# One core, linear attention and mixture of depths: late stores, first steps, gate sums and the last rows rearranged

## The chip, the cores and the metric

The kernel runs on one core of a Trainium2 chip. The metric is the device time of one execution in microseconds (us), lower is better. TensorE (PE) multiplies, its weight loads are shown as PEld; VectorE is DVE, ScalarE is ACT, GpSimd is POOL, and SyncE (SP) only issues transfers. All five run their own instruction queues in program order and wait for each other on semaphores.

## The reference

```python
# attention: B=4 batches, H=8 heads, S=768 positions, D=64, blocks of 64
for b in range(nb):
    intra = einsum('bhic,bhjc->bhij', qb, kb) * Dmask      # Dmask[i,j] = lam**(i-j), i >= j
    intra = einsum('bhij,bhjd->bhid', intra, vb)
    inter = einsum('bhid,bhde->bhie', qb * lam_pow, kv_state)
    out[:, :, sl] = intra + inter
    kv_state = lam_block * kv_state + einsum('bhsd,bhse->bhde', kb * rev_pow, vb)
x = out.transpose(0, 2, 1, 3).reshape(B, S, 512)
# mixture of depths: 128 of the 768 rows of each batch, by score, go through an expert
scores = einsum('bsd,d->bs', x, w_gate)
top_idx = argpartition(-scores[b], capacity)[:capacity]
xe = x[b, top_idx]
out[b, top_idx] = xe + sigmoid(scores[b, top_idx])[:, None] * (relu(xe @ w1) @ w2)
```

All is float32; w1 is 512x1024 and w2 1024x512.

## The kernel before, in words

The sequence is cut into 24 steps g of 128 positions, six to a batch (`NT` = 6). The order of all instructions is written out by hand in one loop over g from -1 to 23; a helper adds the waits. Step g works on the outputs of g and prepares g+1: `transposes(g+1)` turns q and k on PE (ACT copies them out of PSUM), `queries_decayed` and `keys_decayed` scale them on POOL, `scores(g+1)` makes the score blocks in the PSUM tile `su`, `masked` multiplies them by the decay mask on DVE, `state_products` and `next_state` carry the state (`decay_state` scales the old state on POOL), `from_scores(g)` and `from_states(g+1)` accumulate the output in the PSUM tile `o_`, and `outputs(g)` copies it on ACT to `x_b`, from which `store(g)` sends it to DRAM. Steps 0 to 7 are wide (`WIDE` = 8: a state per 128 positions), later ones narrow (two blocks of 64).

Each step also routes: `gate_scores(g)` sums x times the gate vector on DVE, `row` turns the sums into a row (PE, ACT), `compare` fills a table on DVE, `column_sums` counts on PE. When a batch is complete, `find` marks the hits (DVE), `take` makes the token numbers (`tokens`: PE, DVE) and gathers the 128 rows of the batch from DRAM on POOL's queue (`fetch`). Three steps after a batch's last, its expert enters a list of 17 pieces: `gate` (four transposes and a copy `xsT`), eight `hidden` and eight `back`; `products(n)` takes n of them. `finish` makes y and scatters it to DRAM on POOL's queue.

SP's queue holds all loads and stores in program order: at each step the loads of step g+3 (three of 256 KB), then weights (`W1_AT`, `W2_AT`: eight of 512 KB), then the late stores. The outputs of steps 6 to 11 are kept back by

```python
LATE_STORES = {11: (6, 7), 12: (8, 9), 13: (10, 11)}
```

and the fetch of batch 1, in step 13, reads the rows of batches 0 and 1 from DRAM, so it waits for these stores.

Of the kernel before, what the change touches and what calls it, by code (L numbers as in the profile page):

```python
# [17 lines left out]
def kernel(  # L18
# [12 lines left out]
    nc = tc.nc  # L31
# [20 lines left out]
    LATE_STORES = {11: (6, 7), 12: (8, 9), 13: (10, 11)}  # L52
    PIECES = {8: 2, 14: 2, **{g: 2 for g in range(16, 23)}}
# [56 lines left out]

    mask_w = const.tile([128, 2, NHP, L], FP32, name="mask_w")
# [25 lines left out]
    def narrow_constants():  # L137
# [4 lines left out]

    su = psum.tile([128, 2, 512], FP32, name="su")
    o_ = psum.tile([128, 2, 512], FP32, name="o")
    Q_BANK, K_BANK, U_BANK, SMALL = (psum.tile([128, 512], FP32, name=f"m{i}") for i in range(4))
    free = [Q_BANK, K_BANK, U_BANK, SMALL]
    held = []
    nc.vector.memset(
        su[half[1]].rearrange("p a (b i) -> p a b i", i=L)[:, :, :, :C], 0.0
    )  # L150

    def bank(hold=False):
        t = next(t for t in free if not any(t is x for x in held))
        free[:] = [x for x in free if x is not t] + [t]
        if hold:
            held.append(t)
        return t
# [41 lines left out]
    def queries_decayed(g):  # L199
        if g >= NG:  # L200
            return
# [101 lines left out]
    def from_states(g):  # L303
        if g >= NG:
            return
        qs = qss.pop(g)
# [63 lines left out]
    def gate_scores(g):  # L370
        b, t = divmod(g, NT)
        xg = mod.tile([128, HD], FP32, name="xg")
        if wide(g):
            nc.vector.tensor_tensor_reduce(
                out=xg[:].rearrange("p (a m) -> p a m", a=2), in0=o_[:, :, : NHP * D],
                in1=wg_o[:].rearrange("p (a m) -> p a m", a=2),
                scale=1.0, scalar=0.0, op0=ALU.mult, op1=ALU.add,
                accum_out=scs[b][:, t : t + 1],
            )
            return  # L380
# [100 lines left out]
    def expert(b, i):  # L481
# [3 lines left out]
        def gate():  # L485
# [8 lines left out]
            nc.scalar.copy(out=xsT[:].rearrange("p a b -> p (a b)"), in_=pt[:])  # L494
# [55 lines left out]

        return [gate] + [hidden(f) for f in range(NFC)] + [back(f) for f in range(NFC)]
# [7 lines left out]
    wg_o = const.tile([128, HD], FP32, name="wg_o")  # L559

    def gate_vector():
        nc.tensor.matmul(SMALL[:], lhsT=one_row[:], rhs=wg_row[:], start=True, stop=True)
        nc.scalar.copy(
            out=wg_o[:].rearrange("p (a b e) -> p a b e", a=2, e=D),
            in_=SMALL[:].rearrange("p (b a e) -> p a b e", a=2, e=D),
        )
        nc.scalar.copy(out=wg_b[:], in_=SMALL[:])

    def constants():
# [187 lines left out]
```

## Time and profile before

| | us |
|---|---|
| median of 3 timed runs | 194.16 (193.62 to 194.2) |
| the profiled execution's own time | 192.19 |
| its span in the trace | 190.4 |
| PE busy | 160.2 |
| DVE busy, POOL busy, ACT busy | 97.9, 94.2, 71.9 |

The profiled execution is 1.97 us below the median of the timed runs; 1.8 us of its time lie outside the span. Times in the rows below count from the start of the span. A matmul in float32 shows as two instructions.

### The profile page before, as it was taken

What the parts mean: (1) busy time and instruction counts of PE and PEld (TensorE: products, weight loads), DVE (VectorE), ACT (ScalarE), POOL (GpSimd) and SP (SyncE); (2) the same over time, 40 slices, a digit from 0 to 9 for tenths busy, and PEclk for the clock granted to TensorE, in tenths of its full rate; (3) what the DMA queues carried; (4) which work ended last, traced back from release to release, by engine and by line L of the source; (5) the groups of instructions that cost most, each with busy time, mean ns of one, the idle gap of its engine ahead of it and who ended that gap; (6) DMA issues with size and microseconds to landing.
All of it is one profiled execution on the core that took longest, in us unless ns stands there. A gap on an engine that the chain in (4) does not pass through costs nothing.

```text
span 190.4 us, 7792 instructions
## 1 busy us (share of the span) xinstructions
PE 160.2 (84%) x3422; PEld 127.8 (67%) x3422; DVE 97.9 (51%) x227; ACT 71.9 (38%) x193; POOL 94.2 (49%) x103
## 2 busy tenths in 40 slices
PE   0797989999669997999248899997999889989990
PEld 0476879889559896665147789966667779449630
DVE  1946546667746523647052855669665963320000
ACT  2232464453345634523204465544544535012100
POOL 2297646466882743683076384775788400211002
PEclk9999999999999999999957999999999999999996
DMA  5998999998999999999898369898301311011001
GB/s 110 221 218 169 220 213 199 250 222 186 246 314 192 256 293 299 244 257 254 230 254 170 98 129 220 216 242 211 94 34 59 114 59 55 0 55 59 0 0 55
DMA packets 82355, 31.96 MB, mean 168 GB/s; under 512 B 75665, under 2 KB 77713, under 8 KB 82322
## 3 DMA queue, kind: packets, MB, share of 16 engines
q1 hardware_dynamic: 81536, 29.37, 67.2%
q0 software_dynamic: 640, 2.10, 3.3%
q8 instruction: 27, 0.44, 1.0%
q14 instruction: 6, 0.05, 0.1%
q10 hardware_dynamic: 146, 0.01, 0.0%
HBM read 24.12 MB, written 7.34 MB: 165 GB/s over the span
## 4 chain that ended last, share of the span: by engine, by line
PE 38%; issue 17%; DVE 15%; POOL 12%; DMA 10%; ACT 4%; SPq 1%; POOLq 1%; DVEq 0%; ACTq 0%
PE m L530 9%; PE m L518 7%; PE m L192 5%; DVE table L411 4%; POOL decayed L281 4%; PE o L311 4%; PE o L331 3%; DMA xs<-out_dram,tok 3%; PE o L323 2%; PE su L268 2%; POOL kd L176 2%; POOL qs L204 2%; DMA out_dram<-x_b 2%; DMA qn<-in_q_dram 2%; PE su L226 2%
## 5 line engine op out<-in xcount | busy, mean ns | idle before, releaser
L518 PE MATMUL m<-xsT,w_sb 128*128 128x128 f32 x256 | 32.1, 279 | 2.7 <-ACT xsT L494 2.7
L206 POOL TENSOR_TENSOR qs<-qT,qpow 128x512 f32<-128x512 f32 x16 | 21.3, 1328 | 23.5 <-ACT qT L196 23.4
L518 PEld LDWEIGHTS m<-xsT,w_sb 128*128 128x128 f32 x256 | 30.0, 192 | 4.0 <-ACT xsT L494 3.6
L530 PE MATMUL m<-w_sb,hs 128*128 128x512 f32 x64 | 29.7, 598 | 0.0
L411 DVE SCALAR_TENSOR_TENSOR table<-sc_row,sc,lead 128x128 bf16<-128x128 f32 (+5 forms) x24 | 27.0, 1123 | 3.3 <-ACT sc_row L404 3.2
L300 DVE TENSOR_TENSOR state<-su,decayed 128x256 f32<-128x256 f32 x27 | 11.4, 424 | 28.6 <-POOL decayed L281 21.5
L281 POOL TENSOR_TENSOR decayed<-state,decay 128x256 f32<-128x256 f32 x27 | 23.6, 874 | 3.9 <-DVE state L300 2.0
L192 PE MATMUL m<-ident,qn 128*128 128x128 f32 x96 | 16.1, 294 | 6.1 <-DMA qn<-in_q_dram 6.1
L196 ACT COPY qT<-m 128x512 f32<-128x512 f32 x24 | 14.0, 584 | 16.6 <-PE m L192 16.1
L530 PEld LDWEIGHTS m<-w_sb,hs 128*128 128x128 f32 x64 | 11.4, 193 | 9.9 <-issue 9.9
L522 ACT ACTIVATE hs<-m 128x128 f32<-128x128 f32 x32 | 8.9, 279 | 22.5 <-PE m L518 22.5
L311 PE MATMUL o<-state,qs 64*64 64x64 f32 x672 | 16.0, 228 | 1.3 <-ACT x_b L361 0.7
L226 PE MATMUL su<-qT,kT 64*64 64x64 f32 x512 | 10.9, 225 | 7.2 <-DVE state L300 7.2
L176 POOL TENSOR_TENSOR kd<-kn,kpow 128x512 f32<-128x512 f32 x16 | 16.7, 1043 | 0.0
L311 PEld LDWEIGHTS o<-state,qs 64*64 64x64 f32 x672 | 13.1, 138 | 4.9 <-issue 4.0
L204 POOL TENSOR_TENSOR qs<-qT,qpow 128x512 f32<-128x512 f32 x8 | 10.9, 1358 | 10.9 <-ACT qT L196 9.5
L547 POOL DMA_INDIRECT out_dram<-y,tok x4 | 4.2, 1060 | 23.8 <-DVE y L543 23.8
L192 PEld LDWEIGHTS m<-ident,qn 128*128 128x128 f32 x96 | 11.2, 149 | 6.6 <-issue 6.4
L192 PE MATMUL m<-ident,kn 128*128 128x128 f32 x96 | 15.3, 285 | 0.0
L476 POOL DMA_INDIRECT xs<-out_dram,tok x4 | 4.1, 1031 | 22.5 <-DVE tok L459 14.4
L404 ACT COPY sc_row<-m 128x128 f32<-128x128 f32 x24 | 6.4, 267 | 23.2 <-PE m L401 23.2
L226 PEld LDWEIGHTS su<-qT,kT 64*64 64x64 f32 x512 | 9.4, 140 | 7.6 <-DVE state L300 6.3
(79 smaller groups left out, 257.3 us busy)
## 6 DMA issues: line engine op xcount, KB each, us to landing
kn<-in_k_dram SPq DMA_DIRECT2D x24, 256.0 KB, 5.1
qn<-in_q_dram SPq DMA_DIRECT2D x24, 256.0 KB, 5.3
vn<-in_v_dram SPq DMA_DIRECT2D x24, 256.0 KB, 5.6
out_dram<-x_b SPq DMA_DIRECT2D x24, 256.0 KB, 3.8
w_sb<-in_moe_w_dram SPq DMA_DIRECT2D x8, 512.0 KB, 6.1
xs<-out_dram,tok POOLq DMA_INDIRECT x4, 4.3
out_dram<-y,tok POOLq DMA_INDIRECT x4, 3.0
lam_b<-in_lam_dram ACTq DMA_DIRECT2D x1, 4.0 KB, 3.3
```

The costliest lines, as they stand in the source:

```text
L176: nc.gpsimd.tensor_tensor(out=kd[:], in0=loaded[g][0][:], in1=pw[:].rearrange("p a b -> p (a b)").unsqueeze(2).broadcast_to([128, H, D]), ...
L192: nc.tensor.transpose(tp[:, hp * L : (hp + 1) * L], in_=t[:, 2 * hp : 2 * hp + 2, :], identity=ident[:])
L196: nc.scalar.copy(out=dst[:].rearrange("p a i -> p (a i)"), in_=tp[:])
L204: nc.gpsimd.tensor_tensor(out=qs[:], in0=qTs[g][:], in1=qpow[:], op=ALU.mult)
L206: nc.gpsimd.tensor_tensor(out=qs[:].rearrange("p a (c i) -> p a c i", c=2), in0=qTs[g][:].rearrange("p a (c i) -> p a c i", c=2), in1=qpow ...
L226: nc.tensor.matmul(su[half[c], hh, hp * C : (hp + 1) * C], lhsT=kT[half[hh], hp, half[c]], rhs=qT[half[hh], hp, half[c]], start=True, stop ...
L281: nc.gpsimd.tensor_tensor(out=t[:], in0=states[n][:], in1=(decay_w if wide(g) else decay)[:], op=ALU.mult)
L300: nc.vector.tensor_tensor(out=new[:], in0=u, in1=decayed.pop(n)[:], op=ALU.add)
L311: nc.tensor.matmul(o_[half[c if wide(g) else hh ^ c], hh, hp * D : (hp + 1) * D], lhsT=qs[half[hh], hp, half[c]], rhs=states[n][half[hh], ...
L411: nc.vector.scalar_tensor_tensor(out=table[:, : (t + 1) * L], in0=rows_[b][:, : (t + 1) * L], scalar=scs[b][:, t : t + 1], in1=lead[:, (NT ...
L518: nc.tensor.matmul(ph, lhsT=w1_sb[:, dc, f * 128 : (f + 1) * 128], rhs=keep["xsT"][:, dc, :], start=(dc == 0), stop=(dc == NDC - 1),)
L530: nc.tensor.matmul(py[:], lhsT=keep["hs"][:, f, :], rhs=w2_sb[:, f, :], start=(f == 0), stop=(f == NFC - 1),)
```

## The change

The late stores go one step up and ahead of that step's loads. The fetch is split from `take` (as `get`) and stands behind the decay of the state. At the start, 9 matmuls of zeros are issued, `scores(0)` and `masked(0)` go ahead of the first `state_products`, and the gate vector and the routing tables go to later steps; decayed queries of a batch's first wide step are no longer made. In the wide steps the gate sums are taken from the copied rows `x_b` rather than from `o_`, behind `next_state`; `find` goes behind `gate_scores`. Pieces move: none in step 8 but the gate, one more in 14, 20 and 23. The last expert copies `xsT` on two engines and makes and scatters its output in two halves of 256 columns.

```diff
-    LATE_STORES = {11: (6, 7), 12: (8, 9), 13: (10, 11)}
-    PIECES = {8: 2, 14: 2, **{g: 2 for g in range(16, 23)}}
+    LATE_STORES = {10: (6, 7), 11: (8, 9), 12: (10, 11)}
+    PIECES = {8: 0, 14: 2, **{g: 2 for g in range(16, 23)}}
...
+    for _ in range(9):
+        nc.tensor.matmul(SMALL[:, :L], lhsT=zero[:], rhs=zero[:], start=True, stop=True)
...
     def queries_decayed(g):
-        if g >= NG:
+        if g >= NG or (wide(g) and g % NT == 0):
             return
...
     def gate_scores(g):
-        if wide(g):
-            nc.vector.tensor_tensor_reduce(
-                out=xg[:].rearrange("p (a m) -> p a m", a=2), in0=o_[:, :, : NHP * D],
-                in1=wg_o[:].rearrange("p (a m) -> p a m", a=2),
...
         nc.vector.tensor_tensor_reduce(
             out=xg[:], in0=x_bs[b][:, t].rearrange("p a b e -> p (a b e)"), in1=wg_b[:],
...
-            nc.scalar.copy(out=xsT[:].rearrange("p a b -> p (a b)"), in_=pt[:])
+            if last:
+                pv = pt[:].rearrange("p (a b) -> p a b", b=128)
+                nc.scalar.copy(out=xsT[:, : NDC // 2], in_=pv[:, : NDC // 2])
+                nc.vector.tensor_copy(xsT[:, NDC // 2 :], pv[:, NDC // 2 :])
...
+        def half_finish(c):
+            cs = slice(c * (HD // 2), (c + 1) * (HD // 2))
+            y = mod.tile([128, HD // 2], FP32, name="y_half")
+            nc.vector.scalar_tensor_tensor(
+                out=y[:], in0=keep["py"][:, : HD // 2], scalar=keep["g"][:],
+                in1=xss[b, i][:, cs], op0=ALU.mult, op1=ALU.add,
+            )
+            nc.gpsimd.indirect_dma_start(
+                out=rows_upto(b).rearrange("r (c e) -> (r c) e", c=2),
+                out_offset=bass.IndirectOffsetOnAxis(ap=keep["at"][:, c : c + 1], axis=0),
+                in_=y[:], in_offset=None,
+            )
+        if last:
+            after.append(half_rows)
+            return (
+                [gate] + [hidden(f) for f in range(NFC)] + [flush]
+                + [half_back(f, c) for c in range(2) for f in range(NFC)]
+            )
...
     for g in range(-1, NG):
+        for s in LATE_STORES.get(g, ()):
+            store(s)
         loads_to(g + ahead(g))
         for do in weights.get(g, []):
             do()
-        for s in LATE_STORES.get(g, ()):
-            store(s)
...
         if wide(g):
             queries_decayed(g + 1)
+            if g == 0:
+                gate_vector()
             if NGR:
                 compare(g - 1)
-                if ends(g - 2):
-                    take((g - 2) // NT)
             if g >= 0:
                 from_scores(g)
                 outputs(g)
-                gate_scores(g)
                 if g not in kept:
                     store(g)
             if NGR:
+                if ends(g - 2):
+                    take((g - 2) // NT)
+                    get((g - 2) // NT)
                 column_sums(g - 1)
-                if ends(g - 1):
-                    find((g - 1) // NT)
             if g < 0:
-                gate_vector()
-                constants()
-                keys_decayed(1)
+                scores(0)
+                masked(0)
             state_products(g + 1)
             next_state(2 * g + 2)
-            scores(g + 1)
-            masked(g + 1)
+            if g >= 0:
+                gate_scores(g)
+                scores(g + 1)
+                masked(g + 1)
+            if NGR and ends(g - 1):
+                find((g - 1) // NT)
...
+            if g == 0:
+                compare_constants()
             if g == 1:
                 narrow_constants()
+                slot_constants()
+            if g == 3:
+                slot_casts()
             continue
+        if g == NG - 1:
+            products(1)
         from_states(g)
         settle(g)
         queries_decayed(g + 1)
+        if ends(g - 3):
+            for i in range(NGR):
+                pieces.extend(expert((g - 3) // NT, i))
+            if g > WIDE:
+                products(1)
         state_products(g + 1)
         if NGR and ends(g - 2):
             take((g - 2) // NT)
         next_state(2 * g + 2)
         decay_state(2 * g + 3)
+        if NGR and ends(g - 2):
+            get((g - 2) // NT)
         keys_decayed(g + 2)
...
         if NGR:
             column_sums(g - 1)
+        if g == WIDE:
+            products(1)
         outputs(g)
...
         masked(g + 1)
+        gate_scores(g)
         if NGR and ends(g - 1):
             find((g - 1) // NT)
-        gate_scores(g)
         flush()
```

`half_back(f, c)` is `back(f)` for one half of the columns with a PSUM bank of its own per half; `half_rows` makes the row numbers 2*tok and 2*tok+1 on DVE. `compare_constants`, `slot_constants` and `slot_casts` are `constants` cut in three.

## Rows read from the trace of the kernel before

**Rows 1.** Stretches: length, busy us (count) PE, PEld, DVE, ACT, POOL; PEclk; DMA; GB/s.

```profile
20.00:50.00 30.00, 28.27 (x765) 25.10 (x763) 19.17 (x43) 14.32 (x31) 18.49 (x18) 1.00 0.97 223
50.00:97.60 47.60, 37.41 (x903) 29.48 (x895) 21.74 (x54) 18.23 (x54) 26.01 (x26) 0.98 1.07 258
97.60:102.40 4.80, 4.76 (x105) 4.25 (x105) 3.25 (x6) 1.33 (x3) 2.02 (x3) 0.53 1.21 239
102.40:185.20 82.80, 77.32 (x1477) 59.45 (x1473) 41.68 (x97) 32.30 (x97) 36.38 (x36) 1.00 0.38 98
```

**Rows 2.** Timeline, the first 20 us: start, length, instruction, idle time before it.

```profile
6.08 1.09 PE L192 MATMUL m<-ident,qn 128*128 128x128 f32 x4 [6.08 <-DMA qn<-in_q_dram]
...
7.96 2.07 PE L562 MATMUL m<-wg_row,one_row 1*128 1x512 f32 x2
...
8.06 0.59 ACT L196 COPY kT<-m 128x512 f32<-128x512 f32 x1 [0.27 <-PE m L192]
...
11.01 1.98 PE L219 MATMUL su<-qT,kT 64*64 64x128 f32 x32
...
12.66 0.58 DVE L581 CAST slot<-slot_i 128x768 f32<-128x768 int32 x1 [2.43 <-POOL slot_i L578]
...
15.69 1.15 PE L323 MATMUL o<-vn,p 128*64 128x64 f32 x32 [1.47 <-DVE p L236]
...
19.14 0.60 PE L192 MATMUL m<-ident,qn 128*128 128x128 f32 x4
```

**Rows 3.** Timeline of one wide step (g = 3 to 4).

```profile
31.41 1.04 POOL L176 TENSOR_TENSOR kd<-kn,kpow_w 128x512 f32<-128x512 f32 x1
...
32.79 1.23 DVE L236 TENSOR_TENSOR p<-su,mask_w 128x1024 f32<-128x1024 f32 x1
...
34.24 1.01 PEld L323 LDWEIGHTS o<-vn,p 128*64 128x64 f32 x32 [0.17 <-DVE p L236]
```

**Rows 4.** The gate sums' two lines: duration ns min/median/max, first and last start.

```profile
L374 DVE CUSTOM_DVE_ANT_0 xg<-o,wg_o x8: 690/692/692, 17.5 to 50.1; 128x512 f32<-128x512 f32 x8
...
L381 DVE CUSTOM_DVE_ANT_0 xg<-x_b,wg_b x16: 674/682/1754, 59.5 to 159.0; 128x512 f32<-128x512 f32 x16
```

**Rows 5.** Timeline around steps 7 and 8.

```profile
48.33 1.15 PE L323 MATMUL o<-vn,p 128*64 128x64 f32 x32 [0.53 <-DVE p L236]
...
51.33 0.69 PE L226 MATMUL su<-qT,kT 64*64 64x64 f32 x32 [1.22 <-DVE state L300]
...
55.08 0.66 PE L489 MATMUL m<-ident,xs 128*128 128x128 f32 x4 [0.84 <-DMA xs<-out_dram,tok]
```

**Rows 6.** PE's waits over the span: us in total, times, longest.

```profile
PE m L192 <- DMA qn<-in_q_dram: 6.1, 1, 6.1
PE m L518 <- ACT xsT L494: 2.7, 4, 0.7
```

**Rows 7.** Timeline of steps 13 and 14.

```profile
95.39 0.98 POOL L476 DMA_INDIRECT xs<-out_dram,tok  x1 [7.07 <-DMA out_dram<-x_b]
...
97.64 1.13 PE L226 MATMUL su<-qT,kT 64*64 64x64 f32 x32 [5.98 <-DVE state L300]
```

**Rows 8.** The chain that ended last: the last late store, start and length.

```profile
90.76 3.76 DMA out_dram<-x_b
```

**Rows 9.** Timeline of steps 19 and 23, one place each.

```profile
133.00 0.29 PE L401 MATMUL m<-ident,sc 128*128 128x128 f32 x1 [1.23 <-DVE two L457]
...
153.44 0.69 PE L311 MATMUL o<-state,qs 64*64 64x64 f32 x32 [0.71 <-ACT x_b L361]
```

**Rows 10.** Timeline of the end.

```profile
178.15 7.03 PE L530 MATMUL m<-w_sb,hs 128*128 128x512 f32 x16
...
185.22 0.75 DVE L543 SCALAR_TENSOR_TENSOR y<-m,g,xs 128x512 f32<-128x512 f32 x1 [6.12 <-PE m L530]
186.25 0.99 POOL L547 DMA_INDIRECT out_dram<-y,tok  x1 [14.21 <-DVE y L543]
```

**Rows 11.** Page, part 6: gathers of the fetch, median us from issue to landing.

```profile
xs<-out_dram,tok POOLq DMA_INDIRECT x4, 4.3
```

More of the change, by code (lines that the diff above doesn't have):

```diff
@@ L109, with bank @@
     nc.gpsimd.memset(one_row[:], 1.0)
+    su = psum.tile([128, 2, 512], FP32, name="su")
+    o_ = psum.tile([128, 2, 512], FP32, name="o")
+    Q_BANK, K_BANK, U_BANK, SMALL = (psum.tile([128, 512], FP32, name=f"m{i}") for i in range(4))
+    free = [Q_BANK, K_BANK, U_BANK, SMALL]
+    held = []
+    nc.vector.memset(
+        su[half[1]].rearrange("p a (b i) -> p a b i", i=L)[:, :, :, :C], 0.0
+    )
+    def bank(hold=False):
+        t = next(t for t in free if not any(t is x for x in held))
+        free[:] = [x for x in free if x is not t] + [t]
+        if hold:
+            held.append(t)
+        return t
+    for _ in range(9):
+        nc.tensor.matmul(SMALL[:, :L], lhsT=zero[:], rhs=zero[:], start=True, stop=True)
     mask_w = const.tile([128, 2, NHP, L], FP32, name="mask_w")
@@ L141, in narrow_constants @@
         nc.scalar.copy(out=decay[:], in_=qpow[:, :, C - 1 : C].broadcast_to([128, NHP, D]))
[L143 to L157, printed above, removed]
     qTs, qss, kTs, kds, ps_ = {}, {}, {}, {}, {}
@@ L479, in fetch, with expert @@
         xss[b, i] = xs
-    def expert(b, i):
+    def expert(b, i, last=False):
         n_in = min(128, CAP - i * 128)
@@ L549, in finish, with half_back, do, half_rows @@
             )
+        def half_back(f, c):
+            def do():
+                if f == 0:
+                    keep["py"] = bank()
+                nc.tensor.matmul(
+                    keep["py"][:, : HD // 2], lhsT=keep["hs"][:, f, :],
+                    rhs=w2_sb[:, f, c * (HD // 2) : (c + 1) * (HD // 2)],
+                    start=(f == 0), stop=(f == NFC - 1),
+                )
+                if f + 1 == NFC:
+                    half_finish(c)
+            return do
+        def half_finish(c):
[9 more added lines that the diff above has]
+                in_=y[:], in_offset=None,
+            )
+        def half_rows():
+            keep["at"] = at = mod.tile([128, 2], I32, name="half_at")
+            for c in range(2):
+                nc.vector.tensor_scalar(
+                    out=at[:, c : c + 1], in0=toks[b, i][:], scalar1=2.0, scalar2=float(c),
+                    op0=ALU.mult, op1=ALU.add,
+                )
+        if last:
[3 more added lines that the diff above has]
+                + [half_back(f, c) for c in range(2) for f in range(NFC)]
+            )
         return [gate] + [hidden(f) for f in range(NFC)] + [back(f) for f in range(NFC)]
@@ L591, in constants, with slot_casts @@
             )
+    def slot_casts():
+        nc.vector.tensor_copy(slot[:], slot_i[:])
+        nc.vector.tensor_copy(place[:].rearrange("p g c -> p c g"), place_i[:])
     pieces = []
@@ L677 @@
         queries_decayed(g + 1)
+        if ends(g - 3):
+            for i in range(NGR):
+                pieces.extend(expert((g - 3) // NT, i))
+            if g > WIDE:
+                products(1)
         state_products(g + 1)
@@ L682 @@
         decay_state(2 * g + 3)
+        if NGR and ends(g - 2):
+            get((g - 2) // NT)
         keys_decayed(g + 2)
-        if ends(g - 3):
-            for i in range(NGR):
-                pieces.extend(expert((g - 3) // NT, i))
         n = PIECES.get(g, 3)
@@ L690 @@
             row(g - 1)
-        products(1)
+        products(min(n, 1))
         next_state(2 * g + 3)
@@ L695 @@
             compare(g - 1)
-        products(1)
+        products(min(n, 1))
         from_scores(g)
@@ L717 @@
         take(B - 1)
+        get(B - 1)
         products(len(pieces))
@@ L720 @@
         for i in range(NGR):
-            pieces.extend(expert(B - 1, i))
+            pieces.extend(expert(B - 1, i, last=True))
             products(len(pieces))
```

25 lines of the change are left out of this document (9 added, 16 removed).

## The prediction

> **What bounds the kernel now.** I read the stretches first. From the first transposes at 6.08 to the last matmul at 185.2 [rows 2, 10] PE is the engine that does most, and what it loses there is unevenly spread: 1.7 us idle of 30 in the wide steps, 10.2 of 47.6 from 50 on, 5.5 of 82.8 in the late part [rows 1]. In 97.6 to 102.4 PE is full but at a granted clock of 0.53, nearly the lower level of 1.2 GHz [rows 1]. So the kernel is mostly PE's own work with a few holes, and a change pays where it closes one.
>
> Next the timeline, for the holes. The largest is in step 13: POOL waits 7.07 us at 95.39 with the fetch of batch 1, until a store has landed; the decay of the state is queued behind it, the next state behind that, and PE's score products wait 5.98 us for the state [rows 7]. The chain of waits names the store: the last late one, issued at 90.76, landed 3.76 later at 94.52 [rows 8]. Then the start: PE stands until q arrives at 6.08, and the transposes of step 2, the first part of a regular pace, come at 19.14 [rows 2]. Smaller ones stand at steps 7 and 8 [rows 5], before the hidden products (four times 0.7) [rows 6], in steps 19 and 23 [rows 9], and behind the last matmul, where a y of 0.75 and a scatter follow one another [rows 10].
>
> DMA must be kept beside it: 0.97 share in the wide steps and 1.07 from 50 to 97.6 [rows 1]. Up to the stall's end transfers are as full as PE, so what is saved there must not ask for bytes sooner than they can come.
>
> **The change part by part, against the profiled execution's 192.19 us** (span 190.4 and 1.8 around it; the timed median is 1.97 higher).
>
> *Late stores and fetch.* In SP's order the store of step 11 now stands ahead of the loads of steps 15 and 16 and the store of 12, which it used to follow: seven transfers of 256 KB, 1.84 MB, at 258 GB/s [rows 1] 7.1 us. It lands near 94.5 - 7.1 = 87.4 instead of 94.5, before anything is gained earlier. The fetch could go as soon as the token numbers exist, and 95.39 less its wait of 7.07 is 88.3 [rows 7]. So its wait goes; and were 1 or 2 us left, the decay that PE's state needs now stands ahead of it on POOL, with only the keys' decay and the next decay behind. PE's hole of 5.98 closes. With it goes the low clock: 4.76 us of PE work at 0.53 [rows 1] would take about 2.5 at full, 2.3 less. Against that one more piece falls into step 14, a `back`, two of 16 instructions in 7.03 [rows 10], 0.9 us. Sum -7.4. Late next are the loads of steps 13 to 15, behind two, four and six stores, 1.0 us each at that rate: up to 6 us later in the queue. The keys' decay uses them one step after their issue, PE two steps after, so I count nothing, and 4.4 lost at most. Bounds -8.3 and -3.
>
> *The start.* Now 13.06 us pass from the first transposes to those of step 2 (6.08 to 19.14). DVE is held by the cast of the slot table, which itself waited 2.43 us for POOL, and PE's products from scores wait for the masked scores behind it [rows 2]. In the new order the masked scores need besides the decay constants only the score products, and those the second copy, done at 8.65 [rows 2]. At today's speed PE had all its earlier work behind it at 15.69 - 1.47 = 14.22; with the 0.6 that it now waits for the copy that is 14.9 for the products from scores instead of 15.69. At full speed from 8.65 on, score products (1.98 now) and gate vector (2.07 now) take 1.0 each, the next transposes 1.1, the state products 0.6: 12.3. Full speed from 6.08 on moves the copy too: 11.5. That is 0.8, 3.4 and 4.2 earlier, and the rest to step 2 keeps its 3.45. What decides is PE's speed: four transposes take 1.09 at 6.08 and 0.60 at 19.14 [rows 2], although the granted clock is 1.00 in every record of the first stretch. The zero matmuls (18 instructions of 0.22 to 0.27 by the slow row, 4 to 5 us) fit into the 6.08 us in which PE is idle, and give it activity that much sooner. I take -3.0; bounds -4.2 and -0.8.
>
> The Trainium skill (TensorE: Matmul & The Clock Gate, Part 1) says that the throttled clock is the default and that activity releases it; the slow first row agrees, the granted clock shown there does not. By it the zero matmuls bring the fast rows forward and this term lies at its upper end, near -4.
>
> *Gate sums from copied rows.* From `o_` (PSUM) the eight wide sums take 690 to 692 ns, always. The same sum from `x_b`, both inputs in SBUF, takes 682 in the median but 1754 once [rows 4], where it overlapped a POOL multiplication. In a wide step the sum, now behind the state, comes while `kd` runs on POOL to 32.45, so it ends near 33.1 and the masking after it, 1.23 long, at 34.4 instead of 34.0; PE waits for it at 34.24 [rows 3]. That is 0.1 to 0.2 lost per step: +0.7 over seven steps; bounds 0 and +6 (each held as long as the longest shown, 1.07 less the 0.2 of slack).
>
> The Trainium skill (GPSIMD Engine Reference, 1. Specifications) says why: GpSimd shares its SBUF interfaces with VectorE, and they collide where DVE has two SBUF inputs. It speaks against this part, and the one sum of 1754 agrees.
>
> *Tables later.* The cast takes DVE 0.58 [rows 2], the smaller one I put at the same, with a hold of 1.07 at most: 1.2 to 2.2 us once, in step 3, where 1.6 of 4.4 are free (DVE is busy 19.2 of 30 [rows 1]): +0.3; bounds 0 and +0.6. The tables' filling on POOL is covered by POOL's idle time (busy 18.5 of 30 [rows 1]); without it decayed queries would come later by as much.
>
> *Steps 7 and 8.* The masking of 7 no longer stands behind the hits (0.53), the state of step 8 no longer behind a gate sum that waits for its copy (most of 1.22), the gate's transposes come at the end of step 8 and no longer wait for the fetch (0.84), and the first hidden product is a step behind its gate (0.7) [rows 5, 6]: 3.3 at most. But with fewer pieces in step 8 its own chain (decayed queries, decay, state, scores) has less cover, so I take two thirds: -2.2; bounds -3.3 and -1.
>
> *The late steps.* One more wait of 0.7 for `xsT` goes where gate and hidden fall into two steps, and a piece fills the 0.71 in step 23 [rows 6, 9]. The two pieces moved ahead are missing behind the last fetch: a gather lands 4.3 us after its issue [rows 11], six `back` of 0.88 covered it with 5.3 us, and four with 3.5 don't, so 0.8 is lost. Where batches end, gate sum and hits change places; the one behind meets the decayed queries on POOL, and PE waits for it as it did for the other, 1.23 [rows 9]: nothing, by bounds of -2.4 and +1. Sum -0.6; bounds -3 and +1.
>
> *The end.* A half copy of `xsT` saves some 0.25 of the wait of 0.7 [rows 6]; a y of 256 columns takes near half of 0.75 [rows 10], and the first half's scatter goes out 3.5 us before the second. -0.5; bounds -1.0 and 0 (both halves write one tensor, so the second may wait for the first to land).
>
> Sum: -7.4 - 3.0 + 0.7 + 0.3 - 2.2 - 0.6 - 0.5 = -12.7, so 179.5 for a profiled execution, and 194.16 - 12.7 = 181.5 for the median.
>
> **Rivals.** *Transfers give back the early gains.* The start and steps 7 and 8 gain 5.2 us, but DMA is 0.97 busy in the wide steps, 0.9 us free in 30 [rows 1], and full to 97.6. For it: these shares. Against: of all loads only the first ever made PE wait [rows 6]. Then 186.7.
>
> *The wait only changes its place.* Loads that stand behind six stores come late to steps 13 to 15, or the store still lands after the fetch is due. For it: the DMA share of 1.07, a queue that is never empty [rows 1]. Against: the bytes moved behind the store, 7.1 us of them. Then 7.4 becomes about 1 and the time 188.
>
> *It ends slower: the gate sums hold the wide steps.* Each sum could lie behind decayed queries, keys and decay in a row, some 3 us of POOL (`kd` alone 1.04 [rows 3]). It decides when a wide step loses 12.7/8 = 1.6 us; the longest hold shown, 1.07, is not enough [rows 4]. At 2 us a step it is 194.16 - 12.7 + 16 = 197.5. By the Trainium skill's rule on the shared interface it could be so; by the rows it hardly can.
>
> *More is gained.* At batch ends PE's 1.2 us twice [rows 9] goes too, and the start runs at full speed: 177.5.
>
> **How the numbers follow.** Forecast 0.60 (its own range 179 to 184), early gains given back 0.18, wait moved 0.10, more gained 0.09, slower 0.03. The predicted time is 181.5. From 177 to 187 the forecast, the more and most of the given back lie inside, about 0.83. A change within 0.3% (0.6 us) is about what a measurement of this kernel can't tell from none; faster is all but the slower case and 0.01 between: 0.96, 0.01, 0.03.
>
> **What would show it.** In the profile after: the fetch of batch 1 waits under 2 us, and PE's idle time near it stays under 2 with a granted clock of 1.00 throughout; transposes of step 2 at 15 to 17.5, wide steps of 4.4 to 4.6 (sums above 1 us show the held interface); POOL's `kd` in steps 12 to 14 with no wait for a load; behind the last matmul 4.7 instead of 5.2 us. I am wrong if PE waits for loads in steps 9 to 14, if wide steps grow past 5 us, or if the stall stays.

## The result and the profile after

The changed kernel takes 186.77 us in the median of four timed runs (185.32 to 189.67); the kernel before, timed beside it, 194.18. The ratio is 0.961 with a 95% interval of 0.955 to 0.966: faster, by some 4%. The forecast was 181.5, within 177 to 187. So direction and range held, the range by 0.2 us, and the number was 5.3 us too good. The profiled execution takes 185.32 (span 183.5) against 192.19: 6.87 gained where 12.7 were forecast.

Where they went shows when the two traces are cut at the first transposes of a step, in each. Starts are read from the timeline of PE, in us; the last column is the prediction's sum, put on the same stretches. Its -0.6 for the late steps (waits in steps 22 and 23, less the loss behind the last fetch) stands in the last row.

| stretch | before | after | difference | predicted |
|---|---|---|---|---|
| up to the transposes of step 2 | 19.14 | 15.33 | -3.8 | -3.0 |
| steps 1 to 6 | 27.49 | 28.12 | +0.6 | +1.0 |
| steps 7 to 9 | 18.55 | 19.35 | +0.8 | -2.2 |
| steps 10 to 12 | 20.21 | 19.27 | -0.9 | 0 |
| steps 13 and 14 | 21.28 | 14.64 | -6.6 | -7.4 |
| steps 15 to 21 | 40.05 | 44.89 | +4.8 | 0 |
| step 22 and behind | 43.69 | 41.95 | -1.7 | -1.1 |

Two rows carry the miss: steps 7 to 9, 3.0 worse than forecast, and steps 15 to 21, where the sum had nothing but a batch end, put at 0. The -0.9 of steps 10 to 12 lies in step 11, where the trace of the kernel before has a wait of 1.15 us on "issue", of a kind that changes its place from trace to trace (last section); I don't count it as a gain of the change.

The stretches of the changed kernel (the first is steps 1 to 6, then 8 and 9, 13 and 14, 15 to 21; columns as in [rows 1]):

```profile
core 0: us, PE busy (x) PEld busy (x) DVE busy (x) ACT busy (x) POOL busy (x), PEclk, DMA share, GB/s
15.33:43.45 28.12, 26.27 (x694) 23.28 (x694) 21.96 (x43) 13.00 (x28) 20.33 (x23) 1.00 0.99 227
48.17:62.80 14.63, 10.60 (x306) 9.37 (x305) 6.91 (x18) 6.09 (x19) 9.84 (x12) 1.00 1.10 260
82.07:96.71 14.64, 12.59 (x307) 8.97 (x304) 7.72 (x18) 5.93 (x16) 8.86 (x10) 1.00 0.97 230
96.71:141.60 44.89, 40.46 (x1032) 31.66 (x1028) 26.55 (x62) 20.95 (x60) 27.96 (x28) 1.00 0.65 160
```

The granted clock is 1.00 in all four; the 4.76 us at 0.53 that followed the stall [rows 1] have no counterpart. PE is idle 4.0 us of 14.6 in steps 8 and 9, and 4.4 of 44.9 in steps 15 to 21.

The start, against [rows 2] (timeline of PE):

```profile
6.20 0.66 PE L195 MATMUL m<-ident,qn 128*128 128x128 f32 x4 [0.89 <-DMA qn<-in_q_dram]
8.02 1.10 PE L222 MATMUL su<-qT,kT 64*64 64x128 f32 x32 [0.73 <-ACT kT L199]
9.79 0.66 PE L195 MATMUL m<-ident,qn 128*128 128x128 f32 x4
15.33 0.60 PE L195 MATMUL m<-ident,qn 128*128 128x128 f32 x4
```

q still arrives at 6.20, but the first four transposes take 0.66 instead of 1.09 and the score products 1.10 instead of 1.98. Step 13, against [rows 7], first POOL's timeline, then PE's:

```profile
86.71 0.73 POOL L284 TENSOR_TENSOR decayed<-state,decay 128x256 f32<-128x256 f32 x1 [1.98 <-DVE state L303]
87.59 0.99 POOL L471 DMA_INDIRECT xs<-out_dram,tok  x1
```

```profile
85.60 0.30 PE L447 MATMUL m<-place,hit 128*128 128x2 bf16 x6 [1.37 <-DVE hit L437]
```

The fetch goes 0.15 us after the decay, with no wait for a store where it had 7.07. What PE still waits for in this step is 1.37 for the hits. One load does come late: in step 12 POOL's `kd` waits 0.66 us for its keys, at 80.03, where the prediction expected no such wait.

Steps 8 and 9 on PE, against [rows 5, 6], with POOL's part of step 8 in the second fence:

```profile
50.51 0.69 PE L271 MATMUL su<-vn,kd 64*64 64x64 f32 x32 [0.68 <-DVE state L303]
53.69 0.69 PE L229 MATMUL su<-qT,kT 64*64 64x64 f32 x32 [2.01 <-DVE state L303]
56.99 0.27 PE L314 MATMUL o<-state,qs 64*64 64x64 f32 x2 [0.92 <-ACT x_b L364]
```

```profile
50.54 0.73 POOL L284 TENSOR_TENSOR decayed<-state,decay 128x256 f32<-128x256 f32 x1 [0.54 <-DVE state L303]
51.23 1.27 POOL L209 TENSOR_TENSOR qs<-qT,qpow 128x512 f32<-128x512 f32 x1
52.45 0.72 POOL L284 TENSOR_TENSOR decayed<-state,decay 128x256 f32<-128x256 f32 x1
```

A narrow step needs two states in a row, each a decay on POOL and a sum on DVE, and the decayed queries stand between. With no piece in step 8 but the gate at its end, PE waits for the chain twice.

Steps 15 to 21 lose time in two ways. On POOL the scatter of batch 0 now comes ahead of the decayed queries of step 16; on PE two waits end on "issue", that is on nothing that the profile shows another engine do:

```profile
99.19 1.22 POOL L547 DMA_INDIRECT out_dram<-y,tok  x1 [2.83 <-DVE y L543]
100.44 1.28 POOL L209 TENSOR_TENSOR qs<-qT,qpow 128x512 f32<-128x512 f32 x1
```

```profile
104.56 0.20 PE L421 MATMUL m<-ones,table 128*128 128x1 bf16 x2 [0.95 <-DVE table L406]
116.06 0.21 PE L229 MATMUL su<-qT,kT 64*64 64x64 f32 x1 [0.80 <-issue]
122.38 0.33 PE L229 MATMUL su<-qT,kT 64*64 64x64 f32 x4 [0.84 <-issue]
```

The end, against [rows 10] (timeline, chosen rows of PE, ACT, DVE and POOL):

```profile
163.74 0.63 PE L484 MATMUL m<-ident,xs 128*128 128x128 f32 x4 [0.72 <-DMA xs<-out_dram,tok]
164.40 0.37 ACT L491 COPY xsT<-m 128x256 f32<-128x256 f32 x1 [8.28 <-PE m L484]
164.81 0.42 DVE L492 COPY xsT<-m 128x256 f32<-128x256 f32 x1 [1.00 <-ACT xsT L491]
164.83 7.42 PE L518 MATMUL m<-xsT,w_sb 128*128 128x128 f32 x64 [0.46 <-ACT xsT L491]
172.09 7.07 PE L555 MATMUL m<-w_sb,hs 128*128 128x256 f32 x32
179.20 0.48 DVE L567 SCALAR_TENSOR_TENSOR y_half<-m,g,xs 128x256 f32<-128x256 f32 x1 [2.97 <-PE m L555]
179.96 0.97 POOL L571 DMA_INDIRECT out_dram<-y_half,half_at  x1 [2.46 <-DVE y_half L567]
```

From the last matmul (179.16) to the end of the span (183.5) 4.4 us pass instead of 5.2.

### The profile page after: what moved, and what is told of

It is laid out like the page before. It is cut to its first block, busy times and chain, and to the rows that moved or that the text cites. A ratio compares the mean times of both kernels' runs of the same rounds, so it can differ in the third digit from the quotient of the medians.

```text
span 183.5 us, 7853 instructions
## 1 busy us (share of the span) xinstructions
PE 160.5 (87%) x3456; PEld 130.8 (71%) x3456; DVE 99.7 (54%) x231; ACT 70.7 (39%) x192; POOL 95.0 (52%) x102
## 4 chain that ended last, share of the span: by engine, by line
PE 49%; DVE 18%; POOL 13%; issue 9%; DMA 5%; ACT 3%; POOLq 1%; DVEq 0%
PE m L518 13%; PE m L530 9%; PE m L195 5%; POOL decayed L284 5%; DVE table L406 4%; PE o L334 4%; PE o L314 4%; PE su L229 3%; POOL qs L209 3%; DVE xg L376 2%; PE su L271 2%; DVE hit L437 2%; POOL kd L179 2%; PE m L555 2%; DMA xs<-out_dram,tok 2%
## 5 line engine op out<-in xcount | busy, mean ns | idle before, releaser
L209 POOL TENSOR_TENSOR qs<-qT,qpow 128x512 f32<-128x512 f32 x16 | 20.7, 1291 | 24.7 <-ACT qT L199 24.7
L406 DVE SCALAR_TENSOR_TENSOR table<-sc_row,sc,lead 128x128 bf16<-128x128 f32 (+5 forms) x24 | 25.5, 1061 | 5.4 <-ACT sc_row L399 4.8
L303 DVE TENSOR_TENSOR state<-su,decayed 128x256 f32<-128x256 f32 x27 | 11.4, 424 | 22.6 <-POOL decayed L284 14.9
L530 PE MATMUL m<-w_sb,hs 128*128 128x512 f32 x48 | 23.5, 604 | 0.0
L376 DVE CUSTOM_DVE_ANT_0 xg<-x_b,wg_b 128x512 f32<-128x512 f32 x24 | 18.8, 783 | 2.4 <-ACT x_b L364 2.2
L195 PE MATMUL m<-ident,qn 128*128 128x128 f32 x96 | 15.0, 279 | 0.9 <-DMA qn<-in_q_dram 0.9
L195 PE MATMUL m<-ident,kn 128*128 128x128 f32 x96 | 14.4, 273 | 0.0
L199 ACT COPY kT<-m 128x512 f32<-128x512 f32 x24 | 14.2, 591 | 0.0
L179 POOL TENSOR_TENSOR kd<-kn,kpow_w 128x512 f32<-128x512 f32 x8 | 9.8, 1229 | 8.1 <-DVE kpow_w L139 5.2
L334 PEld LDWEIGHTS o<-vn,p 64*64 64x64 f32 x512 | 8.9, 134 | 5.7 <-issue 4.0
L245 DVE TENSOR_TENSOR p<-su,mask 128x512 f32<-128x512 f32 x16 | 11.0, 685 | 3.7 <-PE su L229 3.0
```

What stands on the lines that cost most here:

```text
L179: nc.gpsimd.tensor_tensor(out=kd[:], in0=loaded[g][0][:], in1=pw[:].rearrange("p a b -> p (a b)").unsqueeze(2).broadcast_to([128, H, D]), ...
L195: nc.tensor.transpose(tp[:, hp * L : (hp + 1) * L], in_=t[:, 2 * hp : 2 * hp + 2, :], identity=ident[:])
L199: nc.scalar.copy(out=dst[:].rearrange("p a i -> p (a i)"), in_=tp[:])
L209: nc.gpsimd.tensor_tensor(out=qs[:].rearrange("p a (c i) -> p a c i", c=2), in0=qTs[g][:].rearrange("p a (c i) -> p a c i", c=2), in1=qpow ...
L334: nc.tensor.matmul(o_[half[hh ^ c], hh, hp * D : (hp + 1) * D], lhsT=p[half[c], hh, hp * C : (hp + 1) * C], rhs=vn[half[c], 2 * hp + hh, : ...
L376: nc.vector.tensor_tensor_reduce(out=xg[:], in0=x_bs[b][:, t].rearrange("p a b e -> p (a b e)"), in1=wg_b[:], scale=1.0, scalar=0.0, op0=A ...
```

## The experiments

In each, "the changed kernel" is this one (186.77, ratio 0.961); ratios are to the kernel before, timed beside each run on the same chip. The chips differ (the kernel before has medians of 194.2 to 196.5 on them), so ratios, not medians, compare one run with another.

**1. Late stores alone.** The kernel before with

```diff
-    LATE_STORES = {11: (6, 7), 12: (8, 9), 13: (10, 11)}
+    LATE_STORES = {10: (6, 7), 11: (8, 9), 12: (10, 11)}   # and ahead of loads_to(...)
+        if NGR and ends(g - 2):
+            get((g - 2) // NT)        # the fetch, behind decay_state(2 * g + 3)
```

> The kernel before with one part alone: late stores a step up and ahead of the loads, fetch behind the decay. If the hole of step 13 is worth what the prediction says, 6.0 of PE idle and 2.3 of low clock go: 8.3 us faster (ratio 0.957). Rival, the wait only changes its place (loads behind the stores, or the store still late): 1 to 3 us faster, with PE waiting for a load in steps 12 to 15.

Ratio 0.965 (0.954 to 0.976), profiled 186.07 against 192.19: -6.1, less than the 8.3 expected and far more than the rival's 1 to 3. The part bought nearly the whole gain; what all the rest adds to it (0.961 against 0.965) is within the noise. In step 14 of this run the scatter of batch 0 waits on POOL until the fetched rows have landed, and the step takes 9.22 us; the changed kernel, whose scatter goes out a step later, takes 6.99.

```profile
95.60 1.03 POOL L547 DMA_INDIRECT out_dram<-y,tok  x1 [3.24 <-DMA xs<-out_dram,tok]
```

**2. The new start alone.** The kernel before with

```diff
+    for _ in range(9):
+        nc.tensor.matmul(SMALL[:, :L], lhsT=zero[:], rhs=zero[:], start=True, stop=True)
             if g < 0:
-                gate_vector()
-                constants()
-                keys_decayed(1)
+                scores(0)
+                masked(0)
             state_products(g + 1)     # gate vector and tables in steps 0, 1 and 3
```

> The kernel before with the new first steps alone (zero matmuls, first scores ahead of the state products, tables and gate vector later); gate sums, stores and pieces as before. If the start is PE's own path: transposes of step 2 at 15.3 and 3 to 3.8 us faster at the end (0.981). Rival, transfers give it back: step 2 at 15.3 as well, but the store of step 11 lands no sooner than 94, the fetch waits about 10 instead of 7.07 us, and the time is 0 to 1 us faster.

Ratio 0.998 (0.984 to 1.013): no gain that the timing can tell, though the interval doesn't exclude 3 us. The profiled execution is a long one, 195.5 us where the shortest of the four took 192.49, so it shows one way in which the gain can go, not the usual one. The transposes of step 2 come at 15.32, yet those of step 14 at 87.1, where they were at 85.39. In between PE waits three times on "issue", the longest of them (timeline of PE):

```profile
62.30 0.94 PE L521 MATMUL m<-xsT,w_sb 128*128 128x128 f32 x7 [1.87 <-issue]
```

The other two are 0.95 at 67.8 and 0.65 at 74.5, and from 49.1 to 52.5 the granted clock is 0.51. The last late store, issued at 92.80 instead of 90.76, lands at 96.80 instead of 94.52; the fetch waits 7.63 us and the stall of step 13 stays (6.5 us). So in this execution the 3.8 us gained at the start were gone before the stall. The rival had the time and the late landing right; that transfers were the cause is not shown.

**3. Stores as before, the rest changed.**

```diff
-    LATE_STORES = {10: (6, 7), 11: (8, 9), 12: (10, 11)}
+    LATE_STORES = {11: (6, 7), 12: (8, 9), 13: (10, 11)}   # and behind the loads and weights
```

> The changed kernel with the late stores back a step and behind the loads; the fetch stays behind the decay. If the stores' place is the cause: the fetch waits 6 us or more again and the time is 6 to 8 us over the changed kernel's. Rival, the fetch behind the decay was what counted: the fetch waits as long, but PE's hole stays under 3 us and the time is 0 to 3 us over.

Ratio 0.987 (0.977 to 0.997), median 191.81, 5.0 above the changed kernel and so between the two expectations. With the decay ahead of the fetch, the late store no longer holds the state, and the 6.0 us hole comes back as two smaller ones (timeline of PE):

```profile
96.00 0.69 PE L271 MATMUL su<-vn,kd 64*64 64x64 f32 x32 [1.84 <-POOL kd L179]
98.49 1.09 PE L484 MATMUL m<-ident,xs 128*128 128x128 f32 x4 [1.54 <-DMA xs<-out_dram,tok]
```

The fetch waits 4.8 us for the store again; what stands behind it on POOL (the keys' decay) and its rows themselves come late instead. So the decay ahead of the fetch alone only limits the damage. Early stores with the fetch in its old place were not run.

**4. The old cover of step 8.**

```diff
-    PIECES = {8: 0, ...}
+    PIECES = {8: 2, ...}        # and no gate behind the column sums
```

> The changed kernel with step 8 as before: gate and one hidden product in it, no gate behind its column sums. Theory: taken out of step 8, the pieces uncovered the chain of decay and state, so steps 8 and 9 are 1.5 to 2.5 us shorter here counted with the piece, and the time is about 2 us less (0.99). Rival, PE's work is only moved: the piece saved later is all there is, 0 to 0.5 us.

Ratio 0.985 (0.976 to 0.995), median 191.03: 4 us worse than the changed kernel, against the expectation. The gate now stands where its rows have not landed (timeline of PE):

```profile
53.60 0.66 PE L484 MATMUL m<-ident,xs 128*128 128x128 f32 x4 [2.18 <-DMA xs<-out_dram,tok]
```

The fetched rows land at 53.55. Behind this wait the granted clock is 0.64 from 56 to 63, and step 8 takes 10.63 us. With the early start the old pieces are no cover.

**5. Gate sums from PSUM again**, in their old place ahead of the state:

```diff
+        if wide(g):   # xg from o_[:, :, : NHP * D] and wg_o, then return
```

> The changed kernel with one part undone: the wide steps sum the gate from the PSUM tile, in the old place ahead of the state. Theory A, the price of the copied rows is DVE held while POOL works: the sums of the wide steps, 0.90 to 1.18 us each in the changed kernel, take 0.69 again, and steps 1 to 6 (28.12 us from the transposes of step 2 to those of step 8) shorten by 0.5 to 0.7. Theory B, the wide steps run at the pace of the transfers (DMA share 1.0 and more): they keep 28.1 although the sums are short, and PE waits elsewhere. For the whole time A and B differ little: A gives some 186.1 us, if what is gained is kept behind step 8, and B 186.8, both beside 186.8 for the changed kernel.

Steps 1 to 6 take 27.50 us instead of 28.12, and the difference is that of step 4 (4.42 instead of 5.05): steps 1, 3 and 5 get 0.13 to 0.18 shorter, step 2 gets 0.44 longer, and these cancel. The gate sums by line (min/median/max in ns), of the changed kernel and of this one:

```profile
L376 DVE CUSTOM_DVE_ANT_0 xg<-x_b,wg_b x24: 679/683/1181, 13.9 to 154.0; 128x512 f32<-128x512 f32 x24
```

```profile
L377 DVE CUSTOM_DVE_ANT_0 xg<-o,wg_o x8: 679/692/693, 14.0 to 46.0; 128x512 f32<-128x512 f32 x8
```

That is Theory A's amount, to the tenth, but most of what the short sums save is lost again in step 2. In step 4 the table stands behind the casts that were moved there, and in the changed kernel it runs while POOL multiplies and takes 1.77 us, in this run 0.75 (timeline of DVE; first the changed kernel with POOL's row beside it, then this run):

```profile
30.68 1.27 POOL L207 TENSOR_TENSOR qs<-qT,qpow 128x512 f32<-128x512 f32 x1 [2.13 <-ACT qT L199]
30.73 1.77 DVE L406 SCALAR_TENSOR_TENSOR table<-sc_row,sc,lead 128x512 bf16<-128x512 f32 x1
```

```profile
31.00 0.75 DVE L414 SCALAR_TENSOR_TENSOR table<-sc_row,sc,lead 128x512 bf16<-128x512 f32 x1
```

Step 7 gives 0.5 back, its masking standing behind the sum, and the whole is no faster that a timing can tell: 0.969 (0.963 to 0.975). In this execution the uncovered step 8 had a second price:

```profile
48.00:56.00 8.00, 5.19 (x163) 4.55 (x152) 3.56 (x8) 1.89 (x5) 6.60 (x8) 0.94 1.15 287
56.00:63.00 7.00, 6.91 (x160) 6.28 (x159) 3.38 (x10) 3.75 (x13) 3.68 (x4) 0.83 0.98 216
```

The granted clock falls to 0.83 in that stretch, after PE's two waits in step 8. It does so in runs 6, 8, 11 and 12 too (0.80, 0.82, 0.76 and 0.84 from 56 to 63), in run 3 from 48 to 56 (0.81), and not in runs 7, 9 and 10, nor in the changed kernel's profiled execution, which is 1.4 us faster than its median.

**6. The scatter of y behind the decay** of the next step (where the fetch stands):

```diff
-            nc.gpsimd.indirect_dma_start(out=rows_upto(b), ..., in_=y[:])
+            sends.append(send)     # issued behind get(...), ahead of keys_decayed(g + 2)
```

> The changed kernel, with the scatter of an expert's y issued on POOL one step later behind the decay of the state (where the fetch now stands) rather than ahead of the step's decayed queries. Theory A, step 15 is long because the scatter of batch 0 (1.22 us of POOL at 99.19) stands ahead of the decayed queries and everything behind it on POOL: step 15 falls from 7.96 us to 6.5 to 6.9 and PE's 0.95 for the table goes; the whole time 1.0 to 1.4 us less than the changed kernel, some 185.5. Theory B, the scatter only holds the next thing in line: the keys' decay and the next decay come 1.2 later instead, step 15 stays above 7.5, and the time is the same.

Step 15 falls from 7.96 to 6.76, as A has it, and step 16 takes 7.79 instead of 5.31. A gate sum is held there (timelines of PE, DVE and POOL):

```profile
110.82 0.32 PE L396 MATMUL m<-ident,sc 128*128 128x128 f32 x1 [2.41 <-DVE sc L376]
```

```profile
107.09 3.66 DVE L376 CUSTOM_DVE_ANT_0 xg<-x_b,wg_b 128x512 f32<-128x512 f32 x1
```

```profile
106.25 1.05 POOL L179 TENSOR_TENSOR kd<-kn,kpow 128x512 f32<-128x512 f32 x1
107.25 0.73 POOL L284 TENSOR_TENSOR decayed<-state,decay 128x256 f32<-128x256 f32 x1
107.95 1.26 POOL L209 TENSOR_TENSOR qs<-qT,qpow 128x512 f32<-128x512 f32 x1
109.17 1.03 POOL L179 TENSOR_TENSOR kd<-kn,kpow 128x512 f32<-128x512 f32 x1
```

The sum, 0.68 alone, starts while POOL multiplies and ends 0.55 us after the last of four multiplications without a gap. Ratio 0.966 (0.958 to 0.973): no gain over the changed kernel.

**7. Decayed queries of step 9 on DVE.**

```diff
-            nc.gpsimd.tensor_tensor(
+            (nc.vector if g == 9 else nc.gpsimd).tensor_tensor(
```

> The changed kernel, with the decayed queries of step 9 alone made on DVE instead of POOL. Theory A, step 8 is bound by POOL's chain, now that no expert product covers it: the decayed queries (1.27 us at 51.23) stand ahead of the second decay, so without them PE's wait of 2.01 for the state falls to about 0.8, step 8 from 6.86 to some 5.7, and the whole time by 1.0 to 1.2 us to 185.7. Theory B, transfers set the pace of these steps: the gate then waits for its fetched rows (landing near 52) or later steps for PE's own instructions, and the start of step 11 (62.80) and the whole time stay within 0.4 us.

Step 8 takes 6.57 instead of 6.86: 0.3 where A had 1.2. The decay that now overlaps DVE's 0.68 us multiplication takes 1.11 instead of 0.73, and each state needs the one before, with or without the queries. Then 2.05 and 1.61 us of "issue" waits follow in steps 11 and 12. Median 185.59, ratio 0.959 (0.953 to 0.965): near A's time, but not told apart from the changed kernel's 0.961, and A's way did not occur.

**8. Loads never more than four steps ahead.**

```diff
-        return min(4 + max(0, (g - 12) // 2), AHEAD)
+        return 4
```

> The changed kernel, with loads issued never more than four steps ahead (it lets them run up to eight ahead from step 14 on). Theory A, the waits of 0.80 and 0.84 us in steps 17 and 18, which end on nothing but PE's own issue and lie at multiples of 256 of PE's instructions, are waits for its instruction blocks behind loads that nobody needs yet: with fewer loads in flight DMA's share in steps 15 to 18 falls under 0.9, the two waits vanish, steps 17 and 18 take 5.4 to 5.5 us each, and the whole time is 1.5 us less, some 185.2. Theory B, the blocks wait for something else than the loads: both waits stay, and the time is the same, or up to 2 us more where a load with less lead comes late.

Theory A falls: DMA's share from 98 to 125 goes down to 0.71 to 0.80 (from 0.88 to 0.97), and PE still waits 1.63 on "issue" in step 17. Ratio 0.963 (0.956 to 0.969), the same time.

**9. A quarter of the weights.** Only the first 256 columns of w1 and rows of w2 are loaded, and used four times over.

```diff
-    rhs=w2_sb[:, f, :]
+    rhs=w2_sb[:, f % 2, :]          # the same for w1; loads with i > 0 left out
```

> The changed kernel, loading only the first quarter of the expert's weights (one transfer of 512 KB for each matrix, in steps 6 and 9) and using it four times over, so that its output is another; PE's work is the same and 3.1 MB, some 12 us of transfers at the 258 GB/s of rows 1, are left out between steps 7 and 10. Theory A, transfers take back what the new start gives (PE waits 0.2 to 2 us at a time for its own instruction blocks while DMA is full): with them gone the waits that end on PE's own issue fall from 2.5 us to under 0.8, and DMA's share from step 9 on goes under 0.9; the time is 1.5 to 2.5 us less than the changed kernel, 184.5 to 185.3. Theory B, the shortfall is the chain of step 8, left without a cover: PE's 2.7 us of waits for the state there stay, whatever the transfers, and steps 8 and 9 together keep 14.6 us or more. Both can hold side by side: then A's gain comes and B's waits stay.

Steps 8 and 9 keep 14.66 us and the same waits (0.73, 2.01, 0.92): B holds. DMA's share there is 0.93 instead of 1.10, and from 63 to 84 it falls from 1.07 to 0.68, where PE is busy 20.6 of 21.0 us, as in the changed kernel (20.8). "Issue" waits add up to 2.5 us, now in other places (0.97 in step 1, 0.57 in step 18). Median 184.68, in A's range, ratio 0.956 (0.949 to 0.963), not told apart from 0.961. So the waits of step 8 are not the weights' doing; a small gain elsewhere stays possible.

**10. Step 8 wide as well.**

```diff
-    WIDE = 8
+    WIDE = 9        # the gate of batch 0 at the end of step 8
```

> The changed kernel with step 8 in the wide form too (one state and one decay for its 128 positions instead of two in a row), the gate of batch 0 at its end. Theory A, step 8 is long because two decays and two states follow one another and no expert product lies between: as a wide step it takes 4.8 to 5.2 us instead of 6.86, step 9 keeps 6.6 to 7.8 with its three hidden products and no dip of the granted clock, and the whole time is 1.5 to 2.5 us less than the changed kernel, 184.3 to 185.3. Theory B, the pace there is that of the transfers: step 8 is shorter, but PE then waits for the fetched rows (they land near 52), for loads or for its instruction blocks, and the start of step 12 and the whole time stay within 0.5 us.

Steps 8 and 9 take 4.83 and 6.09 us: 10.9 instead of 14.6, better than A had it. Step 7, which now makes the products of a wide step 8 from its state, takes 5.39 instead of 4.72, so 3.0 are gained over steps 7 to 9. Then one "issue" wait in step 11, with a lower clock behind it, takes most of it back in the profiled execution (timeline of PE; stretches of steps 8 and 9, and 11):

```profile
70.72 0.57 PE L271 MATMUL su<-vn,kd 64*64 64x64 f32 x22 [2.53 <-issue]
```

```profile
49.08:60.01 10.93, 10.22 (x274) 9.32 (x273) 6.58 (x17) 5.23 (x15) 9.66 (x10) 1.00 1.09 264
66.28:76.97 10.69, 8.16 (x162) 6.96 (x162) 3.40 (x8) 3.11 (x10) 3.69 (x4) 0.84 0.91 244
```

Median 184.85, ratio 0.955 (0.949 to 0.962).

**11. Without the zero matmuls.**

```diff
-    for _ in range(9):
-        nc.tensor.matmul(SMALL[:, :L], lhsT=zero[:], rhs=zero[:], start=True, stop=True)
```

> The changed kernel without the nine matmuls of zeros. Theory A, they bring the fast rows forward: without them the first four transposes take 1.1 us instead of 0.66, the products up to the first steps are slow again, and the transposes of step 2 come at 16.5 to 17 instead of 15.33; behind step 8 some of it is given back, so the whole time is 0.5 to 1.5 us more than the changed kernel. Theory B, the new order of the first steps makes the gain and the zeros are idle: step 2 within 0.2 us of 15.33 and the same time.

Theory A (timeline of PE):

```profile
6.30 1.09 PE L192 MATMUL m<-ident,qn 128*128 128x128 f32 x4 [6.30 <-DMA qn<-in_q_dram]
17.36 0.60 PE L192 MATMUL m<-ident,qn 128*128 128x128 f32 x4
```

The first row is slow again and step 2 comes 2.0 us later; the order alone gives 1.8 of the 3.8. Ratio 0.964 (0.956 to 0.972): of the 2.0 no loss is left at the end that the timing can tell.

**12. Runs 5 and 10 together.**

> Step 8 wide, as in the run before it, and the gate sums of all nine wide steps from the PSUM tile in their old place. Theory A, the two savings add up: steps 1 to 7 shorten by some 0.5 us against the wide step 8 alone (33.5 us from the transposes of step 2 to those of step 9), steps 8 and 9 keep 10.9 to 11.3, and the time is 184.0 to 184.6, the fastest so far. Theory B, whatever is gained ahead of step 11 is given back there, as the 2.53 us that PE waited for an instruction block in step 11 of the run before: the start of step 12 stays near 77.0 and the time within 0.3 us of 184.85.

The lowest ratio, 0.949 (0.943 to 0.955), median 184.26: A's time, but not by A's way. Steps 1 to 7 take 32.3 us (A had 33.0), but step 8 is 8.35 long, steps 8 and 9 together 15.4 (A: 10.9 to 11.3), and step 12 starts at 76.86, as B has it. A table is held for 4.27 us and PE waits 2.88 for it (timelines of DVE and POOL):

```profile
48.50 4.27 DVE L414 SCALAR_TENSOR_TENSOR table<-sc_row,sc,lead 128x256 bf16<-128x256 f32 x1
```

```profile
48.55 1.05 POOL L179 TENSOR_TENSOR kd<-kn,kpow 128x512 f32<-128x512 f32 x1
...
51.46 1.03 POOL L179 TENSOR_TENSOR kd<-kn,kpow 128x512 f32<-128x512 f32 x1
```

The same instruction took 0.71 in run 10, where it started at 49.83. In this run it ends 0.28 us after POOL's fourth multiplication in a row, and POOL then stands still for 1.79, waiting for DVE.

## Why the prediction was right, and where it failed

**Late stores and fetch (-7.4): right in mechanism, somewhat too large.** Alone -6.1 (run 1), undone +5.0 in the median (run 3), -6.6 in the stretch. The early stores end the wait, and the low clock goes with it. The -6.6 is not theirs alone: the scatter of batch 0 has left step 14 as well (below).

**The start (-3.0): right in mechanism, 0.8 too small.** -3.8, near the upper end, and the zeros make 2.0 of it (run 11). By the rule of the Trainium skill (TensorE: Matmul & The Clock Gate, Part 1) that activity releases the throttled clock, the prediction put it near -4; the fast first row agrees. The 1.00 that the prediction held against the rule was no measurement: in the traces the records of the granted clock begin, at 1.00, at 13.4 us in the kernel before and at 4.8 in the changed one, where the zeros run from 1.51 on, and the slow rows [rows 2] lie ahead of the first record. But what is gained there isn't kept: alone it shows no gain in the time (run 2).

**Gate sums and tables (+1.0): near in size, +0.6, but not by the way forecast.** Steps 1, 3 and 5 lose 0.13 to 0.18, as forecast, but step 2 gains 0.44. What is left is 0.6 in step 4, from the tables' part (+0.3): there the moved casts push the table into POOL's multiplications, and it takes 1.77 us instead of 0.75 (run 5). That the sum came out near is partly luck.

**Steps 7 and 8 (-2.2): wrong, the step that failed.** The prediction saw that the chain of step 8 has less cover with fewer pieces, and took off a third of 3.3, 1.1 us, for it. Steps 7 to 9 came out at +0.8, so against the 3.3 the loss is 4.1, 3.0 more than the 1.1; and that with one hidden product fewer in them (PE busy 14.5 us instead of 15.1): the sum charged 0.9 for the piece that arrives in step 14 and took nothing off for the one that leaves step 8. PE's idle time in steps 8 and 9 is 4.0 us, and in five of the eight traces with this order of step 8 (the changed kernel, runs 3, 5 to 9 and 11) the granted clock falls in it or behind it. Run 10 shows the cause from the other side: with one state in step 8 instead of two, 3.7 us are gone in steps 8 and 9, 3.0 over steps 7 to 9. Putting the pieces back doesn't help (run 4), since their rows land later than the step needs them. It isn't the weights' transfers (run 9), and hardly the queries on POOL (run 7).

**Steps 15 to 21: 0 in the sum, +4.8.** The prediction followed the pieces into steps 14 and 20 and behind the last fetch, but not the scatter that goes with the last `back`: 1.5 us in step 15, of which run 6 gives back 1.2. Not all of it is lost: before, the same scatter stood in step 14 (at 101.58, ahead of that step's decayed queries). Run 4 has it in step 14 again, and there steps 14 and 15 together take 14.0 us, in the changed kernel 14.9. The two "issue" waits make steps 17 and 18 1.9 longer (runs 10 and 12 have neither wait, and 5.4 to 5.6 us per step). In steps 20 and 21 the gate of batch 2 (0.6) has moved in from step 22. Of the other 0.9, 0.4 is in step 19, the batch end that the prediction put at nothing by bounds of -2.4 and +1; the rest I can't assign.

**The end (-0.5): right in direction, half its size.** Behind the last matmul 0.8 are gained, and the wait for `xsT` is 0.2 shorter: -1.0, the bound. The 0.72 behind the last fetch was forecast as 0.8.

**The rivals.** "Transfers give back the early gains" named the time (186.7) but not the way: PE waits for no load behind the first q, and 3.1 MB fewer transfers change steps 8 and 9 by nothing (run 9). That the time lies in the range is owed to the range having taken in this rival, which did not occur, and so is luck. What took back the start's gain in run 2's profiled execution were 3.5 us of "issue" waits (last section) and a stretch of low clock. "More is gained" adds up to 177.9, not 177.5. "The gate sums hold the wide steps" doesn't happen in the changed kernel, whose longest sum is 1.18; but the hold that I put at 1.07 at most reaches 3.66 and 4.27 in runs 6 and 12. The Trainium skill (SBUF — State Buffer, SBUF: two separate sides) calls the port pair of DVE and GpSimd an exclusive lock in which the loser is blocked for the other's whole instruction. The traces agree that one is held while the other works, and go further: in run 6 the sum waited through four instructions of POOL.

## What to carry to other kernels

A piece of work that is moved takes its tail along: follow the copy, the scatter and the queue that they stand in, not only the matmuls. Before taking filler out of a step, price the dependent chain that it covered, by its hops (here two, each a decay of 0.73 on POOL and a sum of 0.42 us on DVE), and ask whether the chain can be shortened instead: one wide step gained 3.0 us over steps 7 to 9, and putting the pieces back lost time. And read a gain at the start only at the end of the kernel: the same 3.8 us left nothing that the timing could tell while the stall of step 13 stood behind them.

## What the runs showed of the hardware

**PE waits for its own instructions.** The page of the changed kernel shows, of PE and of one DMA queue:

```profile
PE 160.5 (87%) x3456; PEld 130.8 (71%) x3456; DVE 99.7 (54%) x231; ACT 70.7 (39%) x192; POOL 95.0 (52%) x102
q8 instruction: 27, 0.44, 1.0%
```

27 packets of 0.44 MB in all are 16 KB each, and PE has 6,991 instructions in the trace with its weight loads and semaphore waits, a little over 27 times 256. PE's "issue" waits stand at a fixed place in that grid. Counted along these instructions, all waits of 0.25 us and more, of five of the traces:

```
kernel            wait us at PE instruction (and modulo 256)
before            1.15 at 3010 (194)
after             0.49 at 1217 (193), 0.80 at 5057 (193), 0.84 at 5313 (193)
run 2             1.87 at 2497 (193), 0.95 at 2753 (193), 0.65 at 3009 (193), 0.37 at 3957 (117), 0.52 at 5058 (194), 0.30 at 5314 (194)
run 7             2.05 at 3009 (193), 1.61 at 3266 (194), 0.66 at 4290 (194), 0.30 at 5314 (194)
run 10            0.36 at 2041 (249), 2.53 at 3010 (194)
```

Of 34 such waits in 14 traces 32 stand at 193 or 194, and each of the 32 ends 1.27 to 1.73 us after the end of a packet on q8. The Trainium skill (Advanced Engine Details and Errata, ISA Cache) gives a cache line of 16 KB, 256 instructions; the trace agrees. Which block comes late changes from trace to trace, and these waits add up to 0.6 to 4.7 us in each. Of each kernel one execution is traced, so how much of the scatter between executions of one kernel they explain is not shown. That full DMA queues are the reason was not shown: with less traffic, run 8 and run 9 kept waits of up to 1.63 and 0.97. This stays open.

**The two half copies follow one another.** The halves of `xsT` on ACT and DVE need the same transposes, but DVE waits for ACT's half and starts at 164.81, when that is done (164.77). What was gained is the smaller copy (a wait of 0.46 instead of 0.68), not two at once. The reason is a wait in the program: the one semaphore that DVE's half waits for in the trace is raised by ACT's half, at 164.79. Whether the two would run at once without it, no run here tells.
